# A transformer block with modulated norms: the group's copy out of PSUM shared by two engines, two additions of the tail moved, one weight slice's transfers put behind the maxima's rows

## The chip, the cores and the metric

The kernel runs on one core of a Trainium2 chip. Its metric is the time of one execution on the device in microseconds (us), from three runs; a profile of one more execution shows what each engine did. The engines are PE (TensorE: matrix products, with a weight load shown apart as PEld), DVE (VectorE), ACT (ScalarE), POOL (GpSimd) and SP (SyncE, which in this kernel issues every DMA transfer). Products go into PSUM, here 8 banks of 128 x 512 float32; the other engines read them there.

## The reference

One block over 2048 rows x of width 512: attention with 32 heads of width 16, then a dense layer of width 1792 with mish, each behind a layer norm that is scaled and shifted by a vector c, and each added back through a gate.

```python
mod = (_silu(c) @ w_mod).reshape(c.shape[0], 6, 1, -1)
sa, ca, ga, sb, cb, gb = (mod[:, 0], mod[:, 1], mod[:, 2], mod[:, 3], mod[:, 4], mod[:, 5])
h = _layernorm(x, axis=-1) * (1 + ca) + sa
x = x + ga * _A_ref(h, A_wqkv, A_wo)        # softmax(q k / 4) v, 32 heads of 16, then @ wo
h = _layernorm(x, axis=-1) * (1 + cb) + sb
x = x + gb * _B_ref(h, B_w1, B_b1, B_w2)    # mish(h @ w1 + b1) @ w2
```

## The kernel before, in words

**Work and order.** The 2048 queries are cut into four blocks of 512 and the 32 heads into eight groups of four. One block with one group is called an iteration here, n = 0 to 31 (its block is n // 8, its group n % 8). An iteration is 16 steps t, one for each 128 keys. In a step PE makes four score products of iteration n (function `score`, line 512), whose exponential ACT writes (line 520), and four products for the maxima, 20 steps ahead of the scores (`max_tile`, line 471), from which DVE takes the largest score of each row (line 473). Between them stand products of other work, in halves of 64 rows (`mm_half`, line 132): the projections of q, k and v in the first quarter, and the output projection and the MLP of earlier blocks in the rest. Each step ends with the value products of two steps before (`pv`, line 540): eight matmuls, four heads by two halves, that add into one PSUM bank, "acc". Six other banks are a ring that scores, maxima and most other products take in turn; the eighth is called "ms".

**The end of an iteration.** After its last value products `evac(n)` (lines 547 to 586) copies the bank to SBUF as `ot`: one ACT instruction over 128 x 512 (line 554). The next iteration's first value products write the same bank one step later. From `ot` four rows of sums and sixteen rows for each head go to other tiles by DMA (`sm`, `od`, lines 565 and 569).

**The maxima's rows.** When all maxima of iteration n are there, `max_rows` (line 486) turns them on PE, DVE writes them as `mh` and `mt` (lines 494 and 495), and four small DMAs carry `mt` into rows 48 and 49 of the q operand `qa` (line 501). So the products of the scores subtract the maximum, and the first score of n waits for these rows.

**What sets the order.** Each step has two half steps h = 2t and 2t + 1, and a table of hooks says what is issued in which: `at(h, f)` enters f. The rows of iteration n go out at half step 32n - 5, that is, at 27 of the 32 half steps of the group before ("group 5" below means half steps 160 to 191; its rows are those of n = 6). The kernel also turns each slice of the weights w1, wo and w2 into a high and a low part once and stores both in DRAM (`prep_unit`, line 647): a load `hl` (line 653), three POOL operations five half steps later, and nine more half steps later the transfer that stores it (line 660: w1scr, woscr or w2scr). There are 32 slices. `start_preps` chains them: a slice starts no sooner than the store of the third slice before it (of the second, while fewer buffers are free). `clear(h)` (line 181) shifts the half steps of these stores and of some others: from half step 60 on, one that would fall into 25 to 31 of a group goes to 2 of the next. When the last store is out, the pool of the MLP opens and the loads for block 0 begin (`w` at line 666, rows `y` at line 690). Each engine, and SP's queue of transfers, takes its instructions strictly in the order in which the program issues them.

**The tail.** After the last step `tail` (lines 989 to 1082) finishes block 2's last products and does block 3's MLP. `held` computes two remaining products of block 2's second dense layer into a pair of ring banks and returns, for each, an addition into `y` on DVE (line 889). `put_h` (line 710) makes the operands of the last MLP: ACT writes `hf`, POOL its high part (line 95), DVE the low part by a subtraction (line 98). The products of the last dense layer are at line 1074, the four last additions at 1078.

Of the kernel before, what the change touches and what calls it, by code (L numbers as in the profile page):

```python
# [18 lines left out]
def adaln_block(ctx: ExitStack, tc: tile.TileContext, x, wqkv, wo, w1, b1, w2, c, w_mod, out):  # L19
    nc = tc.nc  # L20
    P = 128
# [5 lines left out]
    FT = F // P  # L27
    TB = 512
# [18 lines left out]
    out = out[0]  # L47
# [132 lines left out]

    def clear(h):

        return h if h < 60 or h % 32 < 25 else h - h % 32 + 34

    def at(h, f):
# [344 lines left out]
    accs = {}  # L530
# [17 lines left out]
    def evac(n):  # L548
        qb, g = divmod(n, G)
        t1 = 16 * (n + 1) + 1  # L550
        if g == 0:
            o_hl[qb] = [ap.tile([P, DK, TB], F32R, tag=f"o_{i}", name="o_hl", bufs=1) for i in range(2)]
        ot = ap.tile([P, TB], F32, tag="ot", name="ot", bufs=1)
        nc.scalar.copy(ot, accs.pop(n))
        if g % 2 == 0:
            st["od"] = ap.tile([P, TB], F32, tag="od", name="od", bufs=1)
            st["rb"] = ap.tile([P, TB], F32, tag="rb", name="rb", bufs=1)
        od, rb = st["od"], st["rb"]
        b = 64 * (g % 2)
        if n == NIT - 1:  # L560
            mst["last"] = (ot, od, rb)
            return
        sm = ap.tile([P, 16], F32, tag="sm", name="sm", bufs=2)
        def sums():
            nc.sync.dma_start(sm, ot[DH::32, :])

        def rows():
            for h in range(4):
                nc.sync.dma_start(od[b + 16 * h:b + 16 * h + 16, :], ot[32 * h:32 * h + DH, :])

        rc = ap.tile([P, 16], F32, tag="rc", name="rc", bufs=2)
        hurry = g == G - 1
        at(2 * t1 + 2, sums)
        at(2 * t1 + (24 if g == 2 else 3), rows)
        at(2 * t1 + (5 if hurry else 12), lambda: nc.vector.reciprocal(rc, sm))
        at(2 * t1 + (6 if hurry else 13), lambda: nc.sync.dma_start(rscr[n], rc))
        at(2 * t1 + (8 if hurry else 17),
           lambda: nc.sync.dma_start(rb[b:b + 64, :], dap(rscr, n * 4 * TB, [[TB, 4], [0, DH], [1, TB]])))
        if g % 2 == 1 or n == NIT - 2:
            r = slice(0, P if g % 2 else 64)  # L580

            oh, ol = o_hl[qb]
            k, d, e = (2 * t1 + 42, 7, 11) if g == 1 else (2 * t1 + 11, 0, 0) if hurry else (2 * t1 + 23, 4, 8)
            at(k, lambda: nc.gpsimd.tensor_mul(od[r], od[r], rb[r]))
            at(k + d, lambda: hi_copy("p", oh[r, g // 2, :], od[r]))
            at(k + e, lambda: lo_sub("p", ol[r, g // 2, :], od[r], oh[r, g // 2, :]))
# [403 lines left out]
    def tail():  # L990
# [34 lines left out]
        def held(js):  # L1025
            t = ring(2)
            fins = []
            for i, j in enumerate(js):
                fins.append(mst["held"](j, t[:, i, :]))
                pe_run()  # L1030
            return fins
# [7 lines left out]
        for k in range(DK):  # L1039
            for i in range(4):  # L1040
                nc.tensor.transpose(accs[k][:, i * P:(i + 1) * P], xn[i][:, k * P:(k + 1) * P], ident)
        for k in range(DK):
            put_h(hh, hl, accs[k], k, True)
        fins += held((6, 7))
        for f in fins:
            f(None)
        for f in held((8, 9)):
            f(None)
        for f in range(6):
            w2s[f] = load_w2(f)  # L1050
        po = [ring(2) for _ in range(2)]
# [3 lines left out]
        for u in range(FT + LAG):  # L1055
            if u < FT:
                acc = free2[:, u // 2 % 2, :] if u % 2 else bank(("ms", "acc")[u // 2 % 2])
                up_mms(acc, w1s.pop(u), hh, hl)
                pe_run()
                if u + 8 < FT:  # L1060
                    w1s[u + 8] = w1_tail(u + 8)
                act[u], stages[u] = mish(u, acc, True)
            for d, ss in ((2, (4, 5, 6, 7, 8)), (1, (2, 3)), (0, (0, 1))):
                if 0 <= u - d < FT:
                    for q in ss:
                        stages[u - d][q]()
            f = u - LAG
            if f >= 0:
                a_h, a_l = act.pop(f)
                w = w2s.pop(f)  # L1070
                for i in range(4):
                    s = slice(i * P, (i + 1) * P)
                    for j, (l, r) in enumerate(((a_h, 0), (a_h, 1), (a_l, 0))):
                        nc.tensor.matmul(po[i // 2][:, i % 2, :], l[:, s], w[:, r, :], start=(f == 0 and j == 0),  # L1074
                                         stop=(f == FT - 1 and j == 2))
                    if f == FT - 1 and i % 2:
                        for q in (i - 1, i):
                            nc.vector.tensor_add(y[q], po[q // 2][:, q % 2, :], y[q])
                            r = 4 * last + q
                            nc.sync.dma_start(out[r * P:(r + 1) * P, :], y[q])  # L1080
                if f + 6 < FT:
                    w2s[f + 6] = load_w2(f + 6)

# [289 lines left out]
```

## Time and profile before

| | |
|---|---|
| three runs | 1697.17, 1700.25, 1701.53 us; median 1700.25 us |
| the profiled execution | 1693.26 us, of which 1691.5 us lie between its first and last instruction (the span) |
| mean granted clock of TensorE | 0.996 of full speed |
| busy in the span | PE 1660.6 us, DVE 1429.9 us, ACT 1327.1 us, POOL 898.0 us |
| DMA | 240.03 MB, mean 142 GB/s |

Times of instructions below count from the start of the span. In a line of the timeline stand the start, the duration (of a run of several: all of them), engine, line, operation, what is written from what, and the number of instructions; in brackets, how long the engine was idle before it and what ended that. Matmuls are pipelined, so their durations overlap and a busy PE need not be a PE at its peak. PEclk is the granted clock in a stretch.

### The profile page before, as it was taken

How to read it: one execution, taken by the hardware profiler on the slowest of the kernel's cores; microseconds unless marked ns; L12 is line 12 of the kernel's file. 1: busy time of each engine (PE TensorE's matmuls, PEld its weight loads, DVE VectorE, ACT ScalarE, POOL GpSimd, SP SyncE). 2: the span in 40 equal slices, each digit the busy share in tenths (PEclk: the TensorE clock that was granted, in tenths of full speed). 3: DMA queues.
4: the chain of work that ended last, by engine and by line, in shares of the span. 5: the costliest groups of instructions: out<-in, count | busy, mean ns of one | idle time of the engine just before them, and what ended most of it. 6: DMA issues, size and time to landing. Idle time of an engine off the chain costs nothing.

```text
span 1691.5 us, 32962 instructions
## 1 busy us (share of the span) xinstructions
PE 1660.6 (98%) x12316; PEld 921.7 (54%) x12316; DVE 1429.9 (85%) x2362; ACT 1327.1 (78%) x2559; POOL 898.0 (53%) x906
## 2 busy tenths in 40 slices
PE   6999999999999999999999999999999999999998
PEld 5755665554435455555555555555555555554687
DVE  6898898887998888988888888889888888881577
ACT  6247777777778898888889898888888898889264
POOL 5155215565504388755525498654535597646432
PEclk9999999999999999999999999999999999999999
DMA  7767457777772342434353644334442535332362
GB/s 249 192 224 215 120 159 213 250 226 226 232 210 63 111 123 74 127 80 149 86 133 74 197 105 99 99 109 123 117 103 79 176 95 131 93 107 82 132 218 74
DMA packets 113992, 240.03 MB, mean 142 GB/s; under 512 B 24048, under 2 KB 49648, under 8 KB 107784
## 3 DMA queue, kind: packets, MB, share of 16 engines
q1 hardware_dynamic: 113832, 237.92, 49.6%
q8 instruction: 97, 1.59, 0.4%
q14 instruction: 63, 0.52, 0.1%
HBM read 179.95 MB, written 51.44 MB: 137 GB/s over the span
## 4 chain that ended last, share of the span: by engine, by line
PE 92%; DVE 3%; DMA 2%; ACT 2%; SPq 1%; issue 1%; POOL 0%; DVEq 0%; ACTq 0%; POOLq 0%
PE bk L540 30%; PE ring L471 23%; PE ring L512 22%; PE bk L132 9%; PE bk L126 3%; PE ring L126 3%; PE ring L1074 2%; DVE mx L473 1%; ACT pr L520 1%; DMA xt<-in_A_x 1%; SPq L318 0%; DMA qa<-mt 0%; PE bk L1006 0%; DMA vg<-vscr 0%; PE ring L842 0%
## 5 line engine op out<-in xcount | busy, mean ns | idle before, releaser
L473 DVE TENSOR_REDUCE mx<-ring 128x1 f32<-128x512 f32 x2048 | 1276.1, 684 | 161.5 <-PE bk L132 104.9
L520 ACT ACTIVATE pr<-ring 128x512 f32<-128x512 f32 x2048 | 1090.2, 605 | 232.0 <-PE bk L132 168.8
L471 PE MATMUL ring<-ka,qa 64*128 64x512 f32 x2048 | 778.7, 427 | 0.5
L512 PE MATMUL ring<-qa,ka 64*128 64x512 f32 x2048 | 723.0, 397 | 7.8 <-ACT pr L520 4.6
L471 PEld LDWEIGHTS ring<-ka,qa 64*128 64x128 f32 x2048 | 366.5, 184 | 407.9 <-DVE mx L473 356.2
L540 PE MATMUL bk<-pr,vg 128*32 128x512 f32 x4096 | 545.9, 605 | 0.0
L512 PEld LDWEIGHTS ring<-qa,ka 64*128 64x128 f32 x2048 | 374.1, 184 | 120.8 <-ACT pr L520 35.6
L132 PE MATMUL bk<-h,w 64*128 64x512 f32 x1008 | 280.7, 410 | 0.0
L132 PE MATMUL bk<-w,a_h 64*128 64x512 f32 x576 | 194.8, 417 | 0.6 <-ACT pr L520 0.4
L132 PEld LDWEIGHTS bk<-h,w 64*128 64x128 f32 x1008 | 171.5, 184 | 5.7 <-ACT pr L520 0.4
L540 PEld LDWEIGHTS bk<-pr,vg 128*32 128x32 f32 x4096 | 81.0, 108 | 125.1 <-issue 117.0
L740 POOL TENSOR_SCALAR ee<-hb 128x512 f32<-128x512 f32 x42 | 62.5, 1488 | 96.7 <-ACT hb L734 88.2
L132 PE MATMUL bk<-w,a_l 64*128 64x512 f32 x288 | 113.7, 395 | 0.0
L770 POOL TENSOR_TENSOR ee<-ee,rr 128x512 f32<-128x512 f32 x42 | 53.9, 1284 | 111.6 <-ACT rr L761 111.4
L132 PEld LDWEIGHTS bk<-w,a_h 64*128 64x128 f32 x576 | 95.3, 185 | 5.2 <-ACT pr L520 1.5
L132 PE MATMUL bk<-w,o_hl 64*128 64x512 f32 x288 | 79.7, 409 | 0.0
L98 POOL TENSOR_TENSOR a_l<-hb,a_h 128x512 fp32r<-128x512 f32 x53 | 71.7, 1354 | 4.4
L893 POOL TENSOR_TENSOR y<-yd,y 128x512 f32<-128x512 f32 x40 | 51.4, 1285 | 35.5 <-ACT yd L892 35.3
L754 POOL TENSOR_SCALAR rr<-ee 128x512 f32<-128x512 f32 x42 | 26.1, 622 | 60.0 <-ACT ee L746 59.9
L132 PE MATMUL bk<-h_h,wl 64*128 64x512 f32 x168 | 57.5, 423 | 0.0
L95 POOL TENSOR_SCALAR a_h<-hb 128x512 fp32r<-128x512 f32 x53 | 36.3, 684 | 39.9 <-DVE hb L768 38.3
L774 POOL TENSOR_TENSOR hb<-hb,rr 128x512 f32<-128x512 f32 x42 | 54.5, 1298 | 3.3
(205 smaller groups left out, 1840.9 us busy)
## 6 DMA issues: line engine op xcount, KB each, us to landing
ka<-kscr SPq DMA_DIRECT2D x124, 384.0 KB
w<-w2scr SPq DMA_DIRECT2D x56, 512.0 KB
w<-w1scr SPq DMA_DIRECT2D x46, 512.0 KB
vg<-vscr SPq DMA_DIRECT2D x32, 552.0 KB
qa<-qscr SPq DMA_DIRECT2D x124, 100.0 KB
kscr<-qh SPq DMA_DIRECT2D x16, 512.0 KB
qscr<-qh SPq DMA_DIRECT2D x32, 256.0 KB
hl<-in_B_w SPq DMA_DIRECT2D x28, 256.0 KB
```

The costliest lines, as they stand in the source:

```text
L98: (nc.gpsimd if eng == "p" else nc.vector).tensor_sub(lo, src, hi.bitcast(F32))
L126: nc.tensor.matmul(acc, l, r, start=start, stop=stop)
L132: i = nc.tensor.matmul(acc, l[64 * g:64 * g + 64], r[64 * g:64 * g + 64], start=start, stop=stop)
L471: nc.tensor.matmul(pm, qt[64 * s:64 * s + 64, qs * P:(qs + 1) * P], kt[64 * s:64 * s + 64, kb * TB:(kb + 1) * TB], start=True, stop=True)
L473: return nc.vector.tensor_reduce(out=mxs[n][:, s, 4 * j + qs, kb:kb + 1], in_=pm, op=ALU.max, axis=AX.X)
L512: nc.tensor.matmul(p_, kt[64 * s:64 * s + 64, kc * P:(kc + 1) * P], qt[64 * s:64 * s + 64, :], start=True, stop=True)
L520: e = nc.scalar.activation(pr, p_, AF.Exp, scale=SCALE)
L540: nc.tensor.matmul(accs[n][32 * h:32 * h + 32, :], vgs[n][:, o:o + 32], pts.pop((t, h)), start=(kc == 0), stop=(kc == 15))
L740: nc.gpsimd.tensor_scalar_min(buf("ee", 2), b["hb"], HCAP)
L770: nc.gpsimd.tensor_mul(ee, ee, rr)
L774: nc.gpsimd.tensor_mul(hb, hb, rr)
L893: nc.gpsimd.tensor_add(y[i], yd, y[i])
```

## The change

Three edits. The names A, B and C for them are used from here on.

A, in `clear`: in group 5 alone, half steps 22, 23 and 24 go to 28, which is behind the rows at 27. This moves one store and, since the slice that follows it starts through `clear` too, one load. Behind them the chain of the slices goes on from other half steps: the last stores are sooner, and the MLP's pool opens one step sooner, at t = 120 instead of 121.

B, in `evac`: DVE copies columns 0 to 255 of the bank, ACT columns 256 to 511.

C, in `tail`: the additions of the first held pair, products 4 and 5, stand ahead of `put_h` instead of behind it; and the four additions of the last products stand each behind its own product instead of two by two.

```diff
     def clear(h):
 
+        if h // 32 == 5 and 21 < h % 32 < 25:
+            return h - h % 32 + 28
         return h if h < 60 or h % 32 < 25 else h - h % 32 + 34
...
         ot = ap.tile([P, TB], F32, tag="ot", name="ot", bufs=1)
-        nc.scalar.copy(ot, accs.pop(n))
+        acc = accs.pop(n)
+        nc.vector.tensor_copy(ot[:, :TB // 2], acc[:, :TB // 2])
+        nc.scalar.copy(ot[:, TB // 2:], acc[:, TB // 2:])
...
+        for f in fins:
+            f(None)
         for k in range(DK):
             put_h(hh, hl, accs[k], k, True)
-        fins += held((6, 7))
-        for f in fins:
-            f(None)
-        for f in held((8, 9)):
-            f(None)
+        for js in ((6, 7), (8, 9)):
+            for f in held(js):
+                f(None)
...
-                    if f == FT - 1 and i % 2:
-                        for q in (i - 1, i):
-                            nc.vector.tensor_add(y[q], po[q // 2][:, q % 2, :], y[q])
-                            r = 4 * last + q
-                            nc.sync.dma_start(out[r * P:(r + 1) * P, :], y[q])
+                    if f == FT - 1:
+                        nc.vector.tensor_add(y[i], po[i // 2][:, i % 2, :], y[i])
+                        r = 4 * last + i
+                        nc.sync.dma_start(out[r * P:(r + 1) * P, :], y[i])
```

The order of the instructions on the engines, as both programs are built, shows the three places. Lines of the changed kernel stand two to four higher. First A, on SP in group 5 before (`vg` is the next group's values, `qscr` a projected q that is stored, `hl` a slice that is loaded, `w2scr` one that is stored, `qa<-mt` the maxima's rows of n = 6):

```order
L458 DMA vg<-vscr 128x1104
L252 DMA qscr<-ql 8x16x512
L252 DMA qscr<-qh 8x16x512 x2
L653 DMA hl<-in_B_w 128x512
L660 DMA w2scr<-hl 128x1024
L501 DMA qa_108<-mt 2x4x128 x2
L501 DMA qa_109<-mt 2x4x128 x2
L294 DMA qa_106<-qscr 50x512 x2
```

and in the changed kernel at the same place:

```order
L460 DMA vg<-vscr 128x1104
L254 DMA qscr<-ql 8x16x512
L254 DMA qscr<-qh 8x16x512 x2
L503 DMA qa_108<-mt 2x4x128 x2
L503 DMA qa_109<-mt 2x4x128 x2
L657 DMA hl<-in_B_w 128x512
L664 DMA w2scr<-hl 128x1024
L296 DMA qa_106<-qscr 50x512 x2
```

The four row transfers have moved ahead of one load and one store. One group later, SP before (the rows are those of n = 7):

```order
L252 DMA qscr<-ql 8x16x512
L252 DMA qscr<-qh 8x16x512 x2
L653 DMA hl<-in_B_w 128x512
L660 DMA w2scr<-hl 128x1024
L501 DMA qa_110<-mt 2x4x128 x2
L501 DMA qa_106<-mt 2x4x128 x2
```

and in the changed kernel:

```order
L254 DMA qscr<-ql 8x16x512
L254 DMA qscr<-qh 8x16x512 x2
L664 DMA w2scr<-hl 128x1024
L657 DMA hl<-in_B_w 128x512
L503 DMA qa_110<-mt 2x4x128 x2
L503 DMA qa_106<-mt 2x4x128 x2
```

The load and the store, here of other slices than before, have changed places, so the rows stand right behind a load. Two groups later the rows of n = 8 go out and the MLP's loads begin (`w` are slices of wo, w1 and w2, `y` rows of x). SP before:

```order
L666 DMA w_5337<-woscr 128x1024
L690 DMA y_5267<-in_A_x 128x512
L501 DMA qa_107<-mt 2x4x128 x2
L501 DMA qa_108<-mt 2x4x128 x2
L666 DMA w_5364<-w1scr 128x1024
L666 DMA w_5374<-w2scr 128x1024
```

and SP in the changed kernel:

```order
L670 DMA w_5317<-woscr 128x1024
L694 DMA y_5252<-in_A_x 128x512
L670 DMA w_5347<-w1scr 128x1024
L670 DMA w_5357<-w2scr 128x1024
L503 DMA qa_107<-mt 2x4x128 x2
L503 DMA qa_108<-mt 2x4x128 x2
```

Here the rows stand behind two loads that came after them before. Then B, on ACT around the copy of n = 20, with what each row waits for (`hb` is an MLP product of an earlier block, `pr` the exponentials):

```order
L734 ACTIVATE hb<-bk,b1c 128x512 [waits PE_49]
L520 ACTIVATE pr_1_1176<-ring 128x512
L520 ACTIVATE pr_1_1183<-ring 128x512 [waits PE_49]
L554 COPY ot<-bk 128x512 [waits DMAHW2_49,DMAHW3_49,DMAHW1_49,DMAHW4_49,DMAHW0_49,PE_49]
L520 ACTIVATE pr_2_1151<-ring 128x512 [waits PE_49]
```

and in the changed kernel:

```order
L738 ACTIVATE hb<-bk,b1c 128x512 [waits PE_49]
L522 ACTIVATE pr_1_1176<-ring 128x512
L522 ACTIVATE pr_1_1183<-ring 128x512 [waits PE_49]
L558 COPY ot<-bk 128x256 [waits DMAHW2_49,DMAHW3_49,DMAHW1_49,DMAHW4_49,DMAHW0_49,DVE_49]
L522 ACTIVATE pr_2_1151<-ring 128x512 [waits PE_49]
```

ACT's copy keeps its place and is half as wide; instead of PE it now waits for DVE, whose own copy of the other half waits for PE. On DVE that copy stands between two runs of the maxima's reductions, as at one of the iterations here:

```order
L475 TENSOR_REDUCE mx<-ring 128x1 [waits PE_49] x20
L557 COPY ot<-bk 128x256 [waits DMAHW4_49,DMAHW3_49,DMAHW5_49,DMAHW2_49,PE_49]
L475 TENSOR_REDUCE mx<-ring 128x1 [waits PE_49] x20
L579 RECIPROCAL rc<-sm 128x16 [waits DMAHW2_49]
```

Nothing else moved on DVE there. Last C, on DVE in the tail before (`y` the additions of held products, `h` the subtractions of `put_h`):

```order
L889 TENSOR_TENSOR y_5265<-ring,y_5265 128x512
L889 TENSOR_TENSOR y_5266<-ring,y_5266 128x512
L98 TENSOR_TENSOR h_17735<-hf_17766,h_17734 128x512
L98 TENSOR_TENSOR h_17735<-hf_17770,h_17734 128x512
L98 TENSOR_TENSOR h_17735<-hf_17774,h_17734 128x512
L98 TENSOR_TENSOR h_17735<-hf_17778,h_17734 128x512
L889 TENSOR_TENSOR y_5267<-ring,y_5267 128x512
L889 TENSOR_TENSOR y_5268<-ring,y_5268 128x512
L889 TENSOR_TENSOR y_5265<-ring,y_5265 128x512
L889 TENSOR_TENSOR y_5266<-ring,y_5266 128x512
```

and in the changed kernel:

```order
L893 TENSOR_TENSOR y_5250<-ring,y_5250 128x512
L893 TENSOR_TENSOR y_5251<-ring,y_5251 128x512
L893 TENSOR_TENSOR y_5252<-ring,y_5252 128x512
L893 TENSOR_TENSOR y_5253<-ring,y_5253 128x512
L98 TENSOR_TENSOR h_17767<-hf_17800,h_17766 128x512
L98 TENSOR_TENSOR h_17767<-hf_17804,h_17766 128x512
L98 TENSOR_TENSOR h_17767<-hf_17808,h_17766 128x512
L98 TENSOR_TENSOR h_17767<-hf_17812,h_17766 128x512
L893 TENSOR_TENSOR y_5250<-ring,y_5250 128x512
L893 TENSOR_TENSOR y_5251<-ring,y_5251 128x512
```

Two additions are ahead of the four subtractions now. The products on PE are in the same order in both kernels, and so are the last four additions and their transfers.

## The prediction

> **What bounds the kernel.** First the page's busy times, then the length of each step (from one start of the value products to the next, over all 512), then what PE waits for where a step is long.
>
> ```profile
> PE 1660.6 (98%) x12316; PEld 921.7 (54%) x12316; DVE 1429.9 (85%) x2362; ACT 1327.1 (78%) x2559; POOL 898.0 (53%) x906
> ```
>
> PE is the bound: a change counts only where it makes PE's steps shorter or longer. The usual step takes 2.84 us; what is over that is a stall. These are the stretches that the change touches (columns: start and end, length, busy time and count on PE, PEld, DVE, ACT, POOL, then granted clock, DMA share, GB/s):
>
> ```profile
> 384.39:390.67 6.28, 3.79 (x25) 1.75 (x23) 2.85 (x5) 3.56 (x8) 3.74 (x4) 0.89 0.76 190
> 390.67:394.42 3.75, 3.75 (x25) 1.62 (x23) 2.31 (x5) 1.68 (x4) 2.51 (x3) 0.73 0.96 188
> 1604.40:1607.80 3.40, 3.40 (x9) 2.64 (x8) 2.11 (x4) 0.00 (x0) 0.00 (x0) 0.50 0.42 154
> 1604.08:1608.54 4.46, 4.46 (x13) 3.50 (x13) 2.43 (x4) 0.00 (x0) 0.00 (x0) 0.62 0.36 133
> 1608.54:1611.32 2.78, 2.78 (x14) 2.25 (x12) 0.69 (x1) 0.00 (x0) 0.00 (x0) 1.00 0.60 185
> ```
>
> The first two are the steps at the start of n = 6: 6.28 + 3.75 where two usual steps take 5.68, so 4.35 us too much; part of it is a low clock behind the gap (0.89 and 0.73 on average). The last three lie in the tail: twelve products take 4.46 us, at half clock for most of it, and the next twelve 2.78.
>
> **A, the rows of n = 6.** SP, then DVE, then PE:
>
> ```profile
> 376.66 1.53 SPq L252 DMA_DIRECT2D qscr<-qh  x2
> 379.83 0.45 SPq L653 DMA_DIRECT2D hl<-in_B_w  x1
> 380.71 0.67 SPq L660 DMA_DIRECT2D w2scr<-hl  x1
> 381.51 4.63 SPq L501 DMA_DIRECT2D qa<-mt  x4
> ```
> ```profile
> 377.31 0.34 DVE L495 SCALAR_TENSOR_TENSOR mt<-mh,lows,ring 32x128 fp32r<-32x128 f32 x1 [0.28 <-DVE mh L494]
> ```
> ```profile
> 388.43 0.50 PE L512 MATMUL ring<-qa,ka 64*128 64x512 f32 x1 [2.50 <-DMA qa<-mt]
> ...
> 1407.13 0.39 PE L512 MATMUL ring<-qa,ka 64*128 64x512 f32 x1
> ```
>
> The rows are ready at 377.65, SP has issued qscr by 378.19, and then a load and a store stand ahead, so the rows go out from 381.51 only. In the changed kernel they follow qscr directly: 3.3 us sooner. If all behind them shifts as much, the first score could start at 385.1. It is due at 385.7, 1.33 us after the value products at 384.39: that is where it stands in the step that begins at 1405.80 (its row is the second). The stall goes with 0.6 us to spare, and with it the half clock: -4.35. What is late next are the same rows two groups later, which now stand behind two more loads:
>
> ```profile
> 472.74 2.92 SPq L501 DMA_DIRECT2D qa<-mt  x4
> 476.11 0.33 SPq L666 DMA_DIRECT2D w<-w1scr  x1
> ```
> ```profile
> w<-w1scr SPq DMA_DIRECT2D x46, 512.0 KB
> ```
> ```profile
> 479.89 0.49 PE L512 MATMUL ring<-qa,ka 64*128 64x512 f32 x1
> ```
>
> Before, the last of these rows went out at 475.66, 4.23 us ahead of the score; at n = 6 it took 2.29 us from there (386.14) to the score, so some 1.9 us are to spare. Two loads more are 1.05 MB; but all loads begin one step, 2.84 us, sooner. With 190 GB/s, as in the steps at n = 6, 0.54 MB of that is gone by then and the rest takes 2.7 us; with the 343 GB/s that the step of n = 3 below shows, 0.97 MB is gone and the rest takes 0.2. So a stall of 0 to 0.8 us; I take 0.25, nearer the low end, since large slices go here and not rows of 4 KB. The moved store and load cost nothing: only POOL's splitting of slices waits for them, and that chain ends a step sooner as a whole. A: -4.1.
>
> **B, the copy.** The length of an iteration's last step, in which the bank is copied (n = 3, 8, 20, 27, 29):
>
> ```profile
> 297.95:301.22 3.27, 3.27 (x25) 1.60 (x23) 2.91 (x5) 3.08 (x8) 0.91 (x1) 1.00 1.00 343
> 530.48:533.53 3.05, 3.05 (x24) 1.57 (x23) 2.70 (x5) 3.05 (x9) 0.19 (x1) 1.00 0.01 3
> 1083.07:1086.10 3.03, 3.03 (x25) 1.57 (x23) 2.70 (x5) 3.03 (x8) 2.95 (x3) 1.00 0.59 187
> 1405.80:1408.64 2.84, 2.84 (x25) 1.52 (x23) 2.50 (x5) 2.66 (x6) 2.66 (x3) 1.00 0.08 14
> 1497.16:1500.11 2.95, 2.95 (x24) 1.57 (x22) 2.61 (x5) 2.95 (x8) 2.87 (x3) 1.00 0.02 3
> ```
>
> and ACT at n = 3, 20 and 27:
>
> ```profile
> 299.61 0.62 ACT L91 CAST wh<-wr 128x512 fp32r<-128x512 f32 x1
> 300.13 2.06 ACT L520 ACTIVATE pr<-ring 128x512 f32<-128x512 f32 x4
> ```
> ```profile
> 1083.54 1.10 ACT L520 ACTIVATE pr<-ring 128x512 f32<-128x512 f32 x2
> 1084.50 0.62 ACT L554 COPY ot<-bk 128x512 f32<-128x512 f32 x1
> 1084.96 2.12 ACT L520 ACTIVATE pr<-ring 128x512 f32<-128x512 f32 x4
> ```
> ```profile
> 1406.94 0.59 ACT L554 COPY ot<-bk 128x512 f32<-128x512 f32 x1
> 1407.56 0.60 ACT L520 ACTIVATE pr<-ring 128x512 f32<-128x512 f32 x1
> ```
>
> What lengthens the step is the first exponential behind the copy, which frees a bank of the ring. Counted from the step's start it begins at +1.76 in n = 27 and costs nothing, at +1.89 in n = 20 and costs 0.19, at +2.18 in n = 3 and costs 0.43: about 0.83 us for each us later. n = 27 stands for eight iterations (1, 4 to 7, 11, 19, 27), where ACT is idle when the bank is done at +1.14; n = 20 for nineteen with MLP work ahead on ACT (8 to 10, 12 to 18, 20 to 26, 28, 29; first and last shown), 0.09 to 0.21 each, 3.0 in all; n = 3 for three (0, 2, 3) with a cast behind the copy, 1.2 in all. The last two iterations have no full step behind them. So the copies cost 4.2 us today.
>
> In the changed kernel ACT's copy waits for DVE's. The prices:
>
> ```profile
> L892 DVE COPY yd<-bk 128x512 f32<-128x512 f32 x1 | 0.7, 690 | 10.0 <-PE ring L512 10.0
> ```
> ```profile
> 211.79 0.37 ACT L272 COPY vq<-bk 128x256 f32<-128x256 f32 x1
> 212.06 1.09 ACT L520 ACTIVATE pr<-ring 128x512 f32<-128x512 f32 x2
> ```
> ```profile
> 1084.60 2.49 DVE L473 TENSOR_REDUCE mx<-ring 128x1 f32<-128x512 f32 x4 [0.33 <-PE ring L471]
> ```
>
> DVE has no copy of 128x256 out of PSUM in the trace: it lies between half of 690 ns and all of it. ACT's half takes 0.37 where its whole takes 0.62, six tenths, so I take 0.42. It waits for the bank until +1.14 (the four reductions of the next step queue behind it, whose banks PE's maxima take again), ends at +1.56 and fills the 0.33 us in which DVE idles ahead of its next reduction, so DVE itself is late by 0.1 at most, which the next gap takes up. Then 0.05 until ACT sees it (from the end of a DVE addition, 1603.34 + 0.69, to PE's start at 1604.08 in the rows under C), and ACT's half occupies it for 0.27 (211.79 to 212.06): the exponential comes at +1.88 in all 27 iterations, 0.18 each, 4.9 in all against 3.0; in the other three 0.52 for the cast behind it, +2.40, 0.61 each, 1.8 against 1.2. B: 6.7 - 4.2 = +2.5. With DVE at 0.345 it would be +0.7, with 0.69 (+2.15, 0.41 each, 0.84 with the cast) +9.4.
>
> **C, the tail.** DVE and PE:
>
> ```profile
> 1592.68 2.48 DVE L889 TENSOR_TENSOR y<-ring,y 128x512 f32<-128x512 f32 x4
> 1599.11 0.69 DVE L98 TENSOR_TENSOR h<-hf,h 128x512 fp32r<-128x512 f32 x1 [3.96 <-POOL h L95]
> ...
> 1603.34 2.48 DVE L889 TENSOR_TENSOR y<-ring,y 128x512 f32<-128x512 f32 x4
> ```
> ```profile
> 1604.08 0.98 PE L126 MATMUL ring<-w,a_h 128*128 128x512 f32 x2 [2.42 <-DVE y L889]
> ```
>
> Products 8 and 9 take the ring banks of 4 and 5, whose additions stand behind four subtractions; these wait for POOL until 1599.11. Moved ahead, the two additions run in DVE's idle 3.96 us. PE then has no gap of 2.59 us (1601.49, the end of its last product, to 1604.08), and the twelve products behind it take 2.78 instead of 4.46: -2.59 - 1.68 = -4.27. What is late next is the first MLP product, which needs the last subtraction (done 1603.4) and would be reached 2.8 us after 1601.49, at 1604.3: in time. From there to the last additions PE is without a gap, so the gain carries to the end. The last four additions:
>
> ```profile
> 1685.18 2.79 DVE L1078 TENSOR_TENSOR pr<-ring,pr 128x512 f32<-128x512 f32 x4 [0.59 <-PE ring L1074]
> ```
>
> They run back to back from the first product on already; their split costs and brings nothing (0, at most 0.1 either way).
>
> **Sum.** -4.1 - 4.27 + 2.5 = -5.9: 1693.26 becomes 1687.4. The median of the runs lies 7.0 above this execution, and I carry the sum over as it is: 1700.25 - 5.9 = 1694.4. Change smaller than 0.3%, 5.1 us, can't be told from none, so the forecast lies just past that bound. Its own range is 1692.4 to 1697.
>
> **The rivals.** (1) The stall moves. The rows of n = 8 come over 1.9 us later than before; or those of n = 7, which the order now puts directly behind a load `hl` instead of a store, wait as SP did from 378.19 to 379.83, by the place for a slice's buffer. Each us beyond the spare costs one, and with 2.5 of it the half clock follows as at n = 6: +4.35, 1698.7. For it speaks the 2.7 above; against it that the loads start sooner, and that the row transfers at n = 6 needed 4.63 us to issue besides, where those of n = 8 took 2.92.
>
> (2) The two copies run side by side. Then ACT's half ends its hold at +1.41, ahead of +1.76, and 27 copies cost nothing, three 0.25 each: 0.8 against 4.2, so B is -3.4 and the time 1688.5. Against it stands the wait for DVE in the changed kernel's order. The Trainium skill, page "PSUM — Partial Sum Buffer", section "PSUM bank collisions raise a hardware error", says that two engines may not touch the same bank and quarter of the partitions at once, reads and disjoint columns included, and that software must order them. By that rule the split can't run side by side and B is a loss; the wait in the order agrees, and no run here has tried it otherwise.
>
> (3) The half clock isn't tied to the gaps and stays: only 2.5 and 2.59 go, B as above, -2.3, 1697.9. For it: two places are few to tell. Against it: both stretches begin within 1 us of a gap of 2.4 to 2.5 us. The Trainium skill, page "TensorE: Matmul & The Clock Gate", Part 1, lets the clock fall after an idle window of about 3.4 us; by that the gaps here were too short to cause it. The granted 0.50 right behind both of them speaks against that, and the row decides.
>
> (4) The other side: B is dear. DVE's copy starts behind the fourth reduction at +1.20 and takes the whole 0.69; then the next reduction, due at +1.53, comes at +1.89, 0.36 late, and the exponential at +2.21, 0.46 a step. If only the latter counts, B is +10.9 and the time 1702.8; if both add up, 0.82 each, 1712. It is slower than before by 0.3% from 0.37 more for each of 30 copies than forecast. For it: DVE is 85% busy and the weight loads wait for its reductions; against it the idle 0.33 in the very place.
>
> **Chances.** Forecast 0.64, two thirds of it past the bound: 0.43 faster, 0.21 same. (1) 0.13: 0.11 same, 0.02 slower. (2) 0.07 faster. (3) 0.06 same. (4) 0.10 slower. Together 0.50 faster, 0.38 same, 0.12 slower. The range 1688.0 to 1699.5 holds the forecast's ends, (2), (3) and most of (1); it leaves out (4) and a little.
>
> **What would show it.** A right: the step at 384.39 is 2.84 long and no score of n = 6, 7 or 8 waits for the rows. B right: ACT's copy starts 0.05 behind DVE's end, steps with a copy take 3.02 in all 27, those of n = 27's kind too. C right: no PE gap near 1601 and no half clock behind it. Wrong: a wait for `qa<-mt` at n = 7 or 8, or a DVE copy well over 0.42.

## The result

| | before | changed |
|---|---|---|
| median of 9 runs | 1697.17 us (1691.92 to 1701.53) | 1703.74 us (1700.21 to 1708.18) |
| ratio | 1 | 1.0040, 95% interval 1.0027 to 1.0054 |
| profiled execution | 1693.26 us | 1703.74 us |
| span, granted clock | 1691.5 us, 0.996 | 1702.0 us, 0.994 |

The changed kernel is slower, by 0.4% or 6.6 us between the medians; forecast were 5.9 us less. The page's busy times hardly differ from those of before, so the difference is in waits:

```profile
PE 1662.6 (98%) x12316; PEld 922.5 (54%) x12316; DVE 1441.6 (85%) x2394; ACT 1322.7 (78%) x2559; POOL 897.6 (53%) x906
```

The step at the start of n = 6 is shorter, as forecast, but three steps later in the program are long that were of the usual length before. The windows of the changed kernel at these four steps (columns as in the prediction):

```profile
390.10:393.93 3.83, 3.15 (x25) 1.54 (x23) 2.67 (x5) 3.06 (x8) 3.08 (x3) 1.00 0.98 311
425.29:434.00 8.71, 4.29 (x25) 2.49 (x23) 3.07 (x6) 3.16 (x7) 2.46 (x3) 0.80 0.79 189
442.70:451.02 8.32, 4.71 (x24) 2.09 (x22) 2.85 (x5) 3.16 (x7) 3.57 (x4) 0.79 0.35 89
451.02:455.35 4.33, 4.33 (x24) 1.92 (x22) 2.48 (x5) 1.79 (x4) 2.69 (x3) 0.62 1.00 196
```

6.28 and 3.75 became 3.83 and 2.85. But 8.71, 8.32 and 4.33 stand where each was 2.84 or 2.83 before: 12.9 us. What PE waited for there:

```profile
430.78 0.76 PE L473 MATMUL ring<-ka,qa 64*128 64x512 f32 x1 [4.42 <-DMA ka<-kscr]
...
447.52 0.79 PE L514 MATMUL ring<-qa,ka 64*128 64x512 f32 x1 [3.32 <-DMA qa<-mt]
```

First a k operand (`ka`, needed for the next group's maxima), then the maxima's rows of n = 7. SP's timeline shows both made late. The k operand, in the changed kernel and then before:

```profile
411.64 0.38 SPq L664 DMA_DIRECT2D w2scr<-hl  x1
415.64 0.33 SPq L657 DMA_DIRECT2D hl<-in_B_w  x1
...
418.06 1.51 SPq L664 DMA_DIRECT2D w2scr<-hl  x1
419.67 3.24 SPq L296 DMA_DIRECT2D qa<-qscr  x2
422.97 0.78 SPq L305 DMA_DIRECT2D ka<-kscr  x2
```
```profile
408.46 0.33 SPq L653 DMA_DIRECT2D hl<-in_B_w  x1
408.89 1.43 SPq L294 DMA_DIRECT2D qa<-qscr  x2
410.38 0.77 SPq L303 DMA_DIRECT2D ka<-kscr  x2
```

From 412.02 to 415.64 SP issues nothing: the next in its queue is the load of a slice, whose place is free only when an earlier slice's store has landed. Counted from the value products of n = 6's first step (397.25 before, 399.76 here) `ka` goes out at +23.2 us, not at +13.1. Of these 10.1 us, 4.6 are longer standing at loads (5.9 us from there to `ka`, 1.3 before). The rest is more and slower issuing (16.5 us instead of 8.1): three stores of slices lie ahead of `ka` where one did, and `qa<-qscr` takes 3.24 us instead of 1.43. The rows of n = 7:

```profile
436.32 0.97 SPq L664 DMA_DIRECT2D w2scr<-hl  x1
444.44 0.34 SPq L657 DMA_DIRECT2D hl<-in_B_w  x1
444.88 2.87 SPq L503 DMA_DIRECT2D qa<-mt  x4
```

The load that the order put directly ahead of them stands from 437.29 to 444.44, 7.15 us, and the rows behind it with it.

The copies. The same five last steps as in the prediction (n = 3, 8, 20, 27, 29), then DVE and ACT at n = 20:

```profile
302.66:306.16 3.50, 3.29 (x24) 1.57 (x22) 3.42 (x6) 2.85 (x8) 0.89 (x1) 1.00 0.99 335
545.62:548.57 2.95, 2.95 (x25) 1.59 (x23) 2.95 (x6) 2.95 (x8) 0.19 (x1) 1.00 0.04 11
1098.00:1100.94 2.94, 2.94 (x24) 1.57 (x22) 2.94 (x6) 2.91 (x8) 2.86 (x3) 1.00 0.60 190
1420.30:1423.24 2.94, 2.94 (x24) 1.56 (x23) 2.94 (x6) 2.34 (x6) 2.66 (x3) 1.00 0.10 17
1511.62:1514.55 2.93, 2.93 (x24) 1.57 (x22) 2.93 (x6) 2.83 (x8) 2.85 (x3) 1.00 0.12 17
```
```profile
1099.13 0.42 DVE L557 COPY ot<-bk 128x256 f32<-128x256 f32 x1
1099.53 2.48 DVE L475 TENSOR_REDUCE mx<-ring 128x1 f32<-128x512 f32 x4
```
```profile
1099.59 0.37 ACT L558 COPY ot<-bk 128x256 f32<-128x256 f32 x1
1099.86 2.07 ACT L522 ACTIVATE pr<-ring 128x512 f32<-128x512 f32 x4
```

The two copies run one after the other: DVE's takes 0.42 and ends at 1099.55, ACT's starts at 1099.59. Steps with MLP work became shorter (3.03 to 2.94 at n = 20), idle ones longer (2.84 to 2.94 at n = 27), those with a cast longer (3.27 to 3.50 at n = 3).

The tail, DVE and PE:

```profile
1610.17 0.69 DVE L893 TENSOR_TENSOR y<-ring,y 128x512 f32<-128x512 f32 x1 [0.35 <-PE ring L126]
1611.58 0.69 DVE L893 TENSOR_TENSOR y<-ring,y 128x512 f32<-128x512 f32 x1 [0.72 <-PE ring L126]
1613.54 0.69 DVE L98 TENSOR_TENSOR h<-hf,h 128x512 fp32r<-128x512 f32 x1 [1.27 <-POOL h L95]
```
```profile
1618.47 0.40 PE L126 MATMUL ring<-w,a_l 128*128 128x512 f32 x1
1618.71 2.96 PE L126 MATMUL bk<-h,ka 128*128 128x512 f32 x12
```

The two additions run ahead of the subtractions, PE goes on without a gap, and from the start of the last value products to the end of the span it takes 116.0 us instead of 120.0.

The whole difference of the two profiled executions, by iterations (from the starts of the value products): up to n = 0 -1.4, n = 0 +5.8, n = 1 to 3 +0.5, n = 4 +1.0, n = 5 -3.5, n = 6 +13.0, n = 7 and 8 -0.5, n = 9 to 30 -0.6, the tail -4.0: +10.5. Of the +5.8 at n = 0, 0.2 is the copy of B at its end; the rest lies ahead of every edit: one wait there for a k operand that the other execution did not have, and half clock behind it.

```profile
141.29 0.76 PE L473 MATMUL ring<-ka,qa 64*128 64x512 f32 x1 [3.10 <-DMA ka<-kscr]
```

In the other profiles below the same wait is 0 to 2.9 us, so it belongs to the execution and not to the change. The profiled execution of before lies 3.9 us below the median of its kernel and that of the changed kernel on it: hence 10.5 between the profiles and 6.6 between the medians. Whether this wait makes up those 3.9 us isn't shown, since only one execution of before was profiled.

### The profile page after: what moved, and what is told of

Its sections match the earlier page's. It is cut to its first block, busy times and chain, and to the rows that moved or that the text cites. A ratio compares the mean times of both kernels' runs of the same rounds, so it can differ in the third digit from the quotient of the medians.

```text
span 1702.0 us, 33044 instructions
## 1 busy us (share of the span) xinstructions
PE 1662.6 (98%) x12316; PEld 922.5 (54%) x12316; DVE 1441.6 (85%) x2394; ACT 1322.7 (78%) x2559; POOL 897.6 (53%) x906
## 3 DMA queue, kind: packets, MB, share of 16 engines
q8 instruction: 97, 1.59, 0.4%
## 4 chain that ended last, share of the span: by engine, by line
PE 89%; DVE 4%; DMA 4%; ACT 2%; issue 1%; SPq 1%; POOL 0%; DVEq 0%; ACTq 0%; POOLq 0%
PE bk L542 28%; PE ring L473 22%; PE ring L514 20%; PE bk L132 9%; PE bk L126 3%; PE ring L126 3%; DVE mx L475 2%; PE ring L1078 2%; DMA ka<-kscr 1%; ACT pr L522 1%; DMA qa<-mt 1%; DMA wma<-in_w_mod 1%; DMA w2scr<-hl 0%; DVE hf L376 0%; PE bk L1010 0%
## 5 line engine op out<-in xcount | busy, mean ns | idle before, releaser
L98 POOL TENSOR_TENSOR wl<-wr,wh 128x512 fp32r<-128x512 f32 (+1 forms) x13 | 17.7, 1364 | 75.2 <-ACT wh L91 70.2
```

What stands on the lines that cost most here:

```text
L98: (nc.gpsimd if eng == "p" else nc.vector).tensor_sub(lo, src, hi.bitcast(F32))
```

## The experiments

The theory from these rows: A alone costs the time. It puts the slices from 24 on two half steps sooner (the last two ten and three), so their loads come closer behind the stores for whose landing they wait; SP stands there, and what is queued behind (operands, rows) goes out late. The rivals: the two copies cost it; such waits differ from one execution to the next, whatever the edit; the number of bytes costs it, whoever waits. All runs beside the kernel before on the same chip. "Over" is the time of n = 4 to 8 beyond 80 usual steps of 2.838 us, in the profiled execution; "ka" is when the k operand goes out in n = 6, counted as above, and behind it how long PE waited for it. Each is read from one execution, which lies up to 3.9 us from the median of its kernel (before 3.9 below it, the last two slices held 3.6 below, B and C 3.1 above, the last row 3.8 above); so smaller differences in "over" mean nothing.

| kernel | median, us | ratio to before | over, us | ka, us |
|---|---|---|---|---|
| before | 1696.02 to 1697.40 in five comparisons | 1 | 5.3 | 13.1, no wait |
| changed | 1703.74 | 1.0040 (1.0027 to 1.0054) | 15.4 | 23.2, 4.4 |
| A | 1707.03 | 1.0063 (1.0051 to 1.0075) | 18.7 | 24.9, 5.0 |
| B and C | 1691.94 | 0.9972 (0.9961 to 0.9983) | 9.5 | 18.7, 0.3 |
| C | 1691.41 | 0.9967 (0.9956 to 0.9979) | 7.1 | 14.7, none |
| C, two transfers moved, no shift | 1694.38 | 0.9984 (0.9975 to 0.9994) | 8.1 | 18.6, 0.4 |
| C and the shift alone | 1700.91 | 1.0025 (1.0013 to 1.0036) | 17.6 | 21.1, 2.6 |
| changed, A in group 6 too | 1701.95 | 1.0031 (1.0018 to 1.0044) | 14.2 | 23.3, 5.1 |
| C, rows of n = 5 to 7 from ACT | 1706.15 | 1.0052 (1.0036 to 1.0067) | 18.1 | 16.4, none |
| C, whole copy on DVE | 1691.51 | 0.9962 (0.9947 to 0.9977) | 7.9 | 15.8, none |
| changed, slices loaded by POOL | 1703.01 | 1.0031 (1.0017 to 1.0046) | 15.1 | 17.3, none |
| C, copy on DVE, slices by POOL | 1689.48 | 0.9956 (0.9937 to 0.9976) | 8.7 | 18.0, none |
| changed, last two slices held | 1696.63 | 1.0004 (0.9992 to 1.0016) | 10.1 | 23.6, 5.6 |
| A, C, copy on DVE, by POOL, held | 1687.45 | 0.9952 (0.9936 to 0.9969) | 9.0 | 18.1, none |

### Each part alone

A alone:

```diff
+        if h // 32 == 5 and 21 < h % 32 < 25:
+            return h - h % 32 + 28
```

> Edit A alone. Theory 1 (the shifted chain): the slices behind the moved one load two half steps sooner, so SP stands longer for their places in group 6, and the k operand and the rows of n = 7 come late: A alone is slower than before by 8 to 12 us, with gaps of PE behind ka<-kscr and qa<-mt of n = 7, and the step at n = 6 much shorter than 6.28. Theory 2 (the two copies cost it): A alone gains some 4 us. Theory 3 (such stalls differ from one execution to the next, whatever the edit): A alone is within 3 us of before.

B and C (this edit and the next against the changed kernel):

```diff
-        if h // 32 == 5 and 21 < h % 32 < 25:
-            return h - h % 32 + 28
```

> Edits B and C without A. Theory 1: faster by some 3 us (C -4.3, B about +0.8 as the steps of the changed kernel show: 0.11 a copy, 0.15 at n = 4 to 6, 0.63 at n = 0, 2, 3), no stall in group 6; the stall of n = 6 stays. Theory 2: slower by 8 us or more. Theory 3: within 3 us either way, with a stall of group 6 as likely as with A.

C alone: without A as above, and with this `evac`.

```diff
-        acc = accs.pop(n)
-        nc.vector.tensor_copy(ot[:, :TB // 2], acc[:, :TB // 2])
-        nc.scalar.copy(ot[:, TB // 2:], acc[:, TB // 2:])
+        nc.scalar.copy(ot, accs.pop(n))
```

> Edit C alone. All theories: -4.3 us, from the gap of 2.42 us and the half clock behind it. Against the run with B and C it prices B: under theory 1 that one is 0.6 to 1 us slower than this one, under theory 2 10 us.

A alone is 0.63% slower, 10.7 us. B with C is 0.28% faster and C alone 0.33%, 5.6 us (3.6 to 7.5). So A costs all of the loss and more, B next to nothing (its steps say +0.9: those of n = 0 to 29 are 0.6 longer in all without n = 7, which adds 0.3), and C brings what it should. The waits of A alone, n = 4 to 7:

```profile
PE ring L514 <- DMA qa<-mt: 5.2, 3, 2.7
PE ring L473 <- DMA ka<-kscr: 5.0, 1, 5.0
```

The theory that such waits differ by execution holds in part: without A, the wait for the rows of n = 6, which the prediction took for 2.50 us and its half clock, was 0.44 us in the run of B and C and 1.62 in that of C; in the former the rows of n = 7 waited 3.3 instead. But a wait for `ka` of 2.6 us or more in n = 6 came in each run that has the shift on SP; in the others it was 0.4 us at most.

### Which half of A

The two transfers moved, the later slices left at the half steps of before (and C):

```diff
+    def behind(h):
+
+        return h - h % 32 + 28 if h // 32 == 5 and 21 < h % 32 < 25 else h
...
-            at(clear(h + 9), lambda: nc.sync.dma_start(scr.rearrange("p v m -> p (v m)"),
+            at(behind(clear(h + 9)), lambda: nc.sync.dma_start(scr.rearrange("p v m -> p (v m)"),
...
-        prep_unit(h, three and turn % 3 == 2, *preps[i])
+        third = three and turn % 3 == 2
+        if behind(h) > h:
+            at(behind(h), lambda: prep_unit(behind(h), third, *preps[i]))
+        else:
+            prep_unit(h, third, *preps[i])
```

> Edit C, and of A only the two transfers: the store and the load of group 5 go behind the rows of n = 6, but every later slice stays at the half steps of before. Theory 1: no stall in group 6, the rows of n = 6 in time or nearly, so 3 to 4 us faster than C alone, some 8 faster than before. If moving the two transfers alone is what hurts group 6 (their load and store then fall into its start), it is slower than C alone. Theory 3: as C alone within 3 us.

The shift without the two transfers (and C): the chain reckons as if the slice had been moved, but it isn't.

```diff
+        book = book or h
-        puts = (*puts, clear(h + 9))[-3 if three else -2:]
-        then = clear(max(h + PREP, puts[0] + 1 if len(puts) > 2 - (not three) else 0))
-        at(then, lambda: start_preps(then, i + 1, turn + 1 if three else 0, puts))
+        puts = (*puts, clear5(book + 9))[-3 if three else -2:]
+        raw = max(book + PREP, puts[0] + 1 if len(puts) > 2 - (not three) else 0)
+        then = clear(raw)
+        at(then, lambda: start_preps(then, i + 1, turn + 1 if three else 0, puts, clear5(raw)))
```

Here `clear5` is A's `clear` and `clear` that of before.

> Edit C, and of A only the shift: the two transfers of group 5 stay ahead of the rows as before, but the slices from group 6 on start at the half steps of A. Theory 1a (the shift costs): PE waits for ka<-kscr at the tenth step of n = 6 by 4 to 5 us and for the rows of n = 7 by 3 as with A, so 8 to 12 us slower than C alone. Theory 1b (the two moved transfers cost, by filling the queue at the start of group 6): as C alone within 2 us.

The shift costs: 0.58% against C alone (1.0025 against 0.9967, each beside its own runs of before), about what A costs in all, though PE waited for `ka` by 2.6 us and not by the 4 to 5 expected. Its waits in n = 4 to 7:

```profile
PE ring L516 <- DMA qa<-mt: 7.4, 4, 2.6
PE ring L475 <- DMA ka<-kscr: 2.6, 1, 2.6
```

The two transfers alone brought no gain but a loss, 0.17% or 2.9 us against C (the two intervals overlap): the rows of n = 6 don't wait any more, those of n = 7 do.

```profile
439.41 0.79 PE L516 MATMUL ring<-qa,ka 64*128 64x512 f32 x1 [3.20 <-DMA qa<-mt]
```

So what A was worth at n = 6 came back one group later, although the order of group 6 was that of before: as I read it, a wait of PE gives the transfers time to catch up, and taking it away leaves the next rows behind a fuller queue. The runs without the shift and with all transfers on SP agree, with the waits for the rows of n = 6 and of n = 7: 2.50 and 0 us before, 1.62 and 0.71 in C alone, 1.88 and 1.57 with the copy on DVE, 0.44 and 3.32 in B and C, 0 and 3.20 here. The gain of 3 to 4 us that theory 1 expected of this run did not come.

### Moving the wait on

The changed kernel with A in group 6 too, so that the load ahead of the rows of n = 7 goes behind them:

```diff
-        if h // 32 == 5 and 21 < h % 32 < 25:
+        if h // 32 in (5, 6) and 21 < h % 32 < 25:
```

> All three edits, with A in group 6 as well as in group 5, so that the load ahead of the rows of n = 7 goes behind them too. Theory 1 (SP stands at a load whose place waits for a store to land, and what is behind it is late): the rows of n = 7 are in time, the wait for ka<-kscr in n = 6 stays, 4 to 6 us faster than the changed kernel. Rival (the transfers themselves are slow, the order on SP matters little): the first score of n = 7 waits for its rows by 2 us or more all the same, and the time is the changed kernel's.

The rows of n = 7 are in time, the wait for `ka` stays, and a new one stands at the rows of n = 8, 3.5 us with half clock behind it, so the time is hardly the better (1.0031 against 1.0040), and the 4 to 6 us of theory 1 did not come. Here the order on SP decided which wait it was, not whether there was one.

```profile
PE ring L473 <- DMA ka<-kscr: 5.1, 1, 5.1
PE ring L514 <- DMA qa<-mt: 3.5, 1, 3.5
```

The rows of n = 5 to 7 issued by ACT (and C):

```diff
-                    nc.sync.dma_start(
+                    (nc.scalar if 5 <= n <= 7 else nc.sync).dma_start(
                         qa[(2 * n + j) % NR][64 * s + 48:64 * s + 50, :].rearrange("v (s q) -> v s q", s=4).bitcast(F32),
```

> Edit C, and the rows of n = 5, 6 and 7 issued by ACT instead of SP, no other transfer moved. Theory 1: they no longer stand behind loads on SP, so none of the three first scores waits (1 to 4 us in C alone's trace at n = 6, under 1 at the others): 3 to 6 us faster than C alone, less what twelve issues take of ACT. Rival (the transfers are slow in flight): the waits stay, no gain.

The gain did not come: no score waits for rows any more, but issuing four transfers takes ACT 4.45 us here and 5.53 and 5.93 us for n = 6 and 7, and PE waits for the exponentials behind them. As these waits give the rows time too, the run decides nothing between the theories; it shows only that this queue is no way out.

```profile
334.74 4.45 ACTq L501 DMA_DIRECT2D qa<-mt  x4
339.23 2.06 ACT L520 ACTIVATE pr<-ring 128x512 f32<-128x512 f32 x4 [4.09 <-DMA woscr<-hl]
```

### Taking the standing away from SP

A further place for a slice, so that no load would have to wait, was not run. But the loads can wait on another engine. The changed kernel, with the loads of the slices issued by POOL:

```diff
-        nc.sync.dma_start(raw.rearrange("p (k m) -> p k m", m=src.shape[-1]) if len(src.shape) == 3 else raw, src)
+        nc.gpsimd.dma_start(raw.rearrange("p (k m) -> p k m", m=src.shape[-1]) if len(src.shape) == 3 else raw, src)
```

> All three edits, and the loads of the slices issued by POOL, which uses them, instead of SP; every transfer stays, and every store, row and operand keeps its place on SP. Theory 1 (SP stands where the place of a slice waits for a store to land, and what is queued behind it goes out late): the waits of PE for ka<-kscr in n = 6 and for the rows of n = 7 vanish or fall under 1 us, 8 to 12 us faster than the changed kernel, 2 to 6 faster than before. Rival (it is the traffic: too many bytes at this place, whoever issues them): both waits stay within a third, the time the changed kernel's. A load on POOL may hold up POOL's own work, which would show as late q projections.

Half of the theory stands. In n = 4, 5 and 6 nothing waits (0.4, 0.5 and 0.3 us over): `ka` goes out at +17.3 and the rows of n = 7 in time. So it was the standing on SP that made these too late. But the time is that of the changed kernel, since n = 7 now loses 13.6 us: ACT waits for the landing of a q projection's store, behind it PE for ACT, and then PE for the rows of n = 8 (4.75 us).

```profile
ACT ql L244 <- DMA qscr<-ql: 7.0, 1, 7.0
PE ring L514 <- ACT pr L522: 6.9, 2, 6.7
```

POOL, then SP, show why that store was late:

```profile
433.06 1.29 POOL L98 TENSOR_TENSOR ql<-ql,qh 128x512 fp32r<-128x512 f32 x1
...
438.79 0.58 POOL L657 DMA_DIRECT2D hl<-in_B_w  x1 [4.44 <-DMA qa<-qscr]
...
446.56 1.28 POOL L661 TENSOR_TENSOR hl<-hl,gate 128x512 f32<-128x512 f32 x1 [1.96 <-DMA hl<-in_B_w]
```
```profile
SPq L664 <- POOL hl L98: 10.7, 1, 10.7
```
```profile
450.81 0.73 SPq L254 DMA_DIRECT2D qscr<-ql  x1
```

What the store takes was written by 434.35, yet it went out at 450.81. SP stood from 439.21 to 449.94 at the store of a slice that POOL had not split yet, for POOL had itself stood 4.44 us ahead of its next load and 1.96 us more for that load to land. So the standing was not gone: it had moved to POOL, and came back to SP through a store, much as the expectation's last sentence has it. The traffic isn't needed to explain this loss.

The last two slices held, that is, at the half steps of before (226 and 230), and so the opening of the MLP's pool, all else as changed:

```diff
         then = clear(max(h + PREP, puts[0] + 1 if len(puts) > 2 - (not three) else 0))
+        then = max(then, {29: 226, 30: 230}.get(i, 0))
```

> All three edits, but the last two slices and the opening of the MLP stay at the half steps of before (226, 230), so that no further slice falls into group 6 and the MLP's loads begin no sooner; slices 24 to 29 keep A's shift. Theory 4 (the queue of transfers is nearly full from n = 4 to n = 7, and the slice that A draws forward into group 6 is what overfills it): the waits for ka<-kscr and for rows fall to some 5 us in all with their half clock, 8 us faster than the changed kernel. Theory 1 (the loads that stand on SP two to three half steps behind the store they wait for): the wait for ka<-kscr in n = 6 stays at 4 to 5 us plus half clock, that for the rows of n = 7 goes, since the load ahead of them is gone: 3 to 5 us faster.

0.04% slower than before, with 1 inside the interval of its ratio, where the changed kernel is 0.40% slower: holding these two is worth some 6 us. What is left is the wait for `ka` (its row below, then half clock: that step and the next are 9.91 and 3.90 us), as theory 1 says; the waits for rows in n = 5 to 8 are gone, as theory 4 says.

```profile
425.25 0.76 PE L473 MATMUL ring<-ka,qa 64*128 64x512 f32 x1 [5.56 <-DMA ka<-kscr]
```

So A's shift costs by two ways: slices 24 to 29 closer behind the stores that their loads wait for, some 5 us (1.0004 here against 0.9972 without A); and one slice more in group 6, with the MLP's loads sooner behind it, some 6. Which of these last two it is was not told apart.

### The copy, and the best of it

The whole copy on DVE, with C:

```diff
-        nc.scalar.copy(ot, accs.pop(n))
+        nc.vector.tensor_copy(ot, accs.pop(n))
```

> Edit C, and the whole copy of the accumulators on DVE, none of it on ACT. If the first exponential behind the copy sets its price, as the prediction has it, the 19 steps with MLP work lose 0.16 each and the three with a cast nearly 0.4: some 3 to 4 us faster than C alone. If the reductions do (rival 4), they come 0.36 late in each of 30 steps: 6 to 11 us slower.

DVE and PE in this run, n = 20:

```profile
1089.26 0.69 DVE L554 COPY ot<-bk 128x512 f32<-128x512 f32 x1
1089.87 2.47 DVE L473 TENSOR_REDUCE mx<-ring 128x1 f32<-128x512 f32 x4
```
```profile
1088.13 1.07 PE L540 MATMUL bk<-pr,vg 128*32 128x512 f32 x8
1091.04 1.07 PE L540 MATMUL bk<-pr,vg 128*32 128x512 f32 x8
```

The copy takes 0.69, the reductions begin at +1.74, 0.21 later than the +1.53 of the prediction, and the step takes 2.91: 0.07 over in each of 30 steps, with or without other work on ACT, 2.1 us in all where the copies before cost 4.1 in the same 30 steps. Against C alone that is 2 us by the steps; the runs (0.9962 against 0.9967 in another comparison) can't tell it.

With C, the copy on DVE and the slices loaded by POOL:

> Edit C, the whole copy of the accumulators on DVE, no A, and the loads of the slices issued by POOL. Theory 1: of the waits for rows in n = 5 to 7 (some 6 us with the half clock in the runs with C) most go, so 4 to 6 us faster than C with the copy on DVE, 10 faster than before. Rival (traffic): as C with the copy on DVE.

And all that helped or was free of loss, with A and the last slices held:

> Edits A and C, the whole copy on DVE, the loads of the slices issued by POOL, and the last two slices and the MLP held as in the run before. Theory 4: what stood against A is gone with both, no wait above 1 us in n = 4 to 7 (8 us of them without A): 10 to 13 us faster than before, and the fastest here. Theory 1 alone: the same for n = 4 to 6, as the waits on SP are gone. If the stretch is bound by its bytes, waits of 4 us or more come back somewhere from n = 4 to 7 and the time is that of C with the copy on DVE.

The two are 0.44% and 0.48% faster than before, short of the 10 us and more that was expected, and neither can be told from C with the copy on DVE (0.9962), as the rival of the first had it. The last has the lowest median here, 1687.45 us, but its interval reaches past the ratio of C alone. A, freed of both of its costs, adds nothing that can be told (0.9952 against 0.9956): some wait for rows remains in each, at n = 5 and 7 in the first and at n = 5 and 8 in the last. What bounds the stretch then, its bytes or the order of its issues, stays open. The last run:

```profile
PE ring L514 <- DMA qa<-mt: 3.1, 2, 2.0
```

## Why the prediction was right or wrong

**A was wrong in sign: -4.1 forecast, +10.7 measured alone.** The local term held roughly: the two steps of n = 6 fell from 10.03 to 6.68 us, where 5.68 was forecast. The rows went out 4.56 us ahead of the first of these steps instead of 2.88, so 1.7 us sooner and not 3.3, since SP came later to the stores ahead of them, and the first score still waited 0.68 us. The step that failed is the sentence "The moved store and load cost nothing: only POOL's splitting of slices waits for them, and that chain ends a step sooner as a whole." That the chain ends sooner was taken for no cost. It is the cost, 0.58% or some 10 us for the shift alone against C: shifted loads stood on SP, and shifted stores were issued, ahead of the k operand of n = 6, which the prediction never looked at (PE waited 4.42 us for it in the changed kernel); and one more slice came into group 6, with the MLP's loads sooner behind it. Of a moved step each transfer that it draws along had to be followed, and each thing queued behind it on SP; the prediction followed the rows alone.

**The stall at n = 6 was taken for a property of the kernel.** It was 2.50 us in the one profile of before, and 1.62, 1.88 and 0.44 in the three runs that left rows and slices as they were; and where it was 0.44, or was taken away cleanly, the rows of n = 7 waited 3.3 and 3.2. The term was right for that execution and not for the kernel.

**Rival 1 had the place.** The rows of n = 7 behind a load waited as it says, 7.15 us on SP, 3.32 on PE and the half clock behind it. It had 0.13, and a price of one stall; there were two, with the half clock each time. The rows of n = 8, on which the sum was spent, were in time in the changed kernel.

**B was right in kind and too dear: +2.5 forecast, some +0.9 by the steps.** The order of the copies, DVE's 0.42 and ACT's start (+1.59 against +1.61 forecast) held, and the exponential comes at +1.86 against +1.88. What failed is the line "about 0.83 us for each us later". It joined n = 20, where the exponentials ahead of the copy are late as well, to n = 3, where they aren't. In the changed kernel the step is longer by just as much, within 0.01, as the exponential comes after +1.757: 0.105 at +1.861 (n = 1), 0.152 at +1.905 (n = 6), 0.625 at +2.380 (n = 0); before, 0.381 at +2.136 (n = 0). By that line +1.88 costs 0.12, not 0.18, +2.40 costs 0.64, and B comes to 27 x 0.12 + 3 x 0.64 - 4.2 = +1.0.

**Rival 2, side by side, didn't happen**, as the wait in the order said. **Rival 4** fails in both parts: DVE's half took 0.42, so the exponential came at +1.86 and not at +2.21; and where DVE makes the whole copy in 0.69, its reductions are 0.21 late and cost 0.07 a step, not 0.36.

**C was right: -4.27 forecast**, -4.0 in the tail of the profile, -5.6 (-3.6 to -7.5) in the runs of C alone. The 2.59 of the sum is a little too much: by the rows the last product ends at 1601.66, and PE is idle for 2.42. The split of the last additions changed nothing: the four take 2.78 us behind 0.59 of idle time, 2.79 and 0.59 before. **Rival 3** fell with it: in the tail, half clock stands in the two profiles with the gap (before and A alone) and in none of the twelve without it.

**The sum** was made on one execution and carried to the median. Waits for transfers differ between executions by as much as the forecast itself (n = 0 alone took from 3.7 to 9.8 us beyond its 16 usual steps in the fourteen profiles), so its own range of 4.6 us was too narrow.

## What to carry to other kernels

Where one queue issues all transfers in order, moving one of them moves whatever its schedule draws along: list every transfer that goes out at another time, and for each what waits behind it, above all loads that wait for a place. Ahead of removing a wait in a stretch whose transfers run close to full, ask which wait comes next: there it gave the queue time, and came back a group later. A price for lateness is read from cases in which only the one thing is late.

## What the runs showed of the hardware

The clock fell behind shorter gaps than the two in the prediction, and not behind each. In C alone a gap of 1.62 us was followed by half clock; in A alone one of 1.86 us (ahead of n = 5) was not. Their steps:

```profile
386.02:391.86 5.84, 4.22 (x25) 2.00 (x23) 2.84 (x5) 3.67 (x8) 3.71 (x4) 0.79 0.81 221
```
```profile
338.67:343.64 4.97, 3.11 (x25) 1.51 (x23) 2.66 (x5) 2.57 (x7) 0.88 (x1) 1.00 0.46 153
```

So the length of a gap alone doesn't tell whether the half clock follows. The Trainium skill, page "TensorE: Matmul & The Clock Gate", Part 1, has the clock follow a window that runs on its own and needs about 3.4 us idle; that the same kind of gap counts at one time and not at another agrees with a window of its own, the length doesn't.

The records of the granted clock show the windows. In every profile here the stretches of half clock that follow such gaps last 3.41 or 6.83 us, and their starts lie whole multiples of 3.41 us apart (140.30, 430.43 and 447.50 in the changed kernel: 85 and 5 of them). Carried on through the execution, this grid cuts it into windows. In C alone the whole gap lies in one window, and the next is at half clock:

```profile
386.02:389.43 3.41, 1.79 (x14) 0.64 (x14) 1.86 (x3) 1.99 (x5) 1.36 (x2) 1.00 0.73 243
389.43:392.84 3.41, 3.41 (x20) 1.56 (x18) 1.96 (x3) 2.28 (x4) 3.33 (x4) 0.50 0.88 196
```

In A alone the gap falls on both sides of a cut at 341.01, with 0.84 us in one window and 1.02 in the next. A gap of even 2.28 us had no half clock behind it (copy on DVE, n = 0), split into 1.40 and 0.88. Between 115 and 1680 us of all fourteen profiles, each window at full clock in which PE was idle for 1.62 us or more was followed by one at half clock, and none with 1.40 or less was; between these lie one of each kind (1.50 with, 1.53 without).

And issuing a small transfer is not free for an engine that computes: four on ACT took 4.45 to 5.93 us, in which no exponential ran.
